# A fused attention and softplus kernel: new positions for all tasks and identity products, and a bank of its own for half of the last tile

## The chip, the cores and the metric

The kernel runs on one core of a Trainium2 chip. The core has TensorE (PE in the profile) with its weight loads (PEld), VectorE (DVE), ScalarE (ACT), GpSimd (POOL) and SyncE (SP, which here only issues DMAs). Matmuls write to PSUM, which the kernel uses as eight banks of 128 partitions x 512 float32 words; DVE and ACT read the banks.

The metric is the device time of one execution in microseconds, as the median of several runs. Lower is better.

## The reference

```python
kv = np.einsum('bhsd,bhse->bhde', k, v)          # B=8, H=8, S=576, D=64
out = np.einsum('bhsd,bhde->bhse', q, kv)
rms = np.sqrt(np.mean(out * out, axis=-1, keepdims=True) + 1e-06)
attn = (out / rms * g_norm).astype(np.float32)
x = attn.transpose(0, 2, 1, 3).reshape(B * S, H * D)      # 4608 x 512
h = x @ w_in                                     # 512 x 2048
g = np.maximum(h, 0.0) + np.log1p(np.exp(-np.abs(h)))     # softplus
return (g @ w_out).astype(np.float32)            # 2048 x 512
```

The weights w_in and w_out come as 64-bit floating point words, all else as 32-bit.

## The kernel before, in words

**Pieces.** A float32 operand is kept as three pieces of fewer bits (a high, a low and a third part, called `high`, `low` and `less` or `third` in the code) that TensorE takes. ACT makes the high part, DVE the two others. A logical product is therefore three matmuls for each 128 rows of depth.

**The head.** The first 60 us or so bring in and convert the first weights. A weight block `j` (even j: 128 columns of w_in, odd j: 128 rows of w_out) is fetched (L423), converted from 64-bit words by five DVE and two ACT operations (L433 to L465), and split into pieces (L498 to L529; for some blocks the third piece comes by way of two products on TensorE, L525 and L526). In the same time k and v are loaded (L683, L685) and multiplied batch by batch into kv (`kv_of`, L696), q tiles are loaded (L766) and transposed on TensorE (`turn_q`, L776), q is multiplied with kv (`out_rows`, L720), the rows are normed (square on ACT, sum on DVE L724, root on POOL L728, product on DVE L732), transposed (`turn_x`, L738), and split into pieces (L640, L643, L646). One of the 36 tiles of 128 rows is called `t`.

**Phase 0.** 64 steps (`step`, L849) follow. A step takes one block of 384 rows and one chunk of 128 hidden columns: 12 matmuls of 384 columns (`mm1`, L864), softplus on ACT (L886), pieces (L888, L875, L879), and three times 3 matmuls of 512 columns (`mm2`, L871) that add to a bank. Attention for later tiles is worked in between.

**Phases 1 and 2.** 48 wide steps (`wide_step`, L1044) take 512 rows and two chunks of hidden columns. The hidden part is made by seven products on half-sized blocks (`multiply`, L1066, 6 matmuls of 256 columns each) with sums between them: copies on ACT (L1091, L1108, L1112) and one DVE addition (L1116) on which the seventh product waits. Softplus (L1094) and pieces (L1124, L1127, L1130) follow, and then eight times 3 matmuls of 512 columns (`mm2`, L1137), for two chunks c and four tiles i. The last step's pieces are made chunk by chunk (L1152, L1154, L1158). In the last step of a block of 512 rows, `leave` (L913) takes each tile's sums out of its bank, scales them and sends them to the output. For the last tile of all, `leave` does this in two halves: `left` on ACT (L921), `right` on DVE (L924), both into the one output tile `ot`, followed by one DMA for each half (L928 on SP, L929 on ACT).

**What sets the order.** The program's order is written by a planner in Python (`Plan.order`) when the kernel is built. Every operation is a task with an engine, a nominal duration, the tasks that it depends on, the buffers that it takes and gives back, and a position. Where several tasks of an engine can start at about the same nominal time, the planner takes the one with the lowest position. The resulting lists are the instruction streams of the engines; each engine then runs its own in order. The positions come from lists of numbers: P0 for the weight blocks (conversion, fetch), P4 for the tiles' attention, P5 for k, v and q of the batches, P7 for single loads of k, v and q in the head, P1 and P2 for the later weights, P3 for the order inside a wide step.

**Identity products.** Where the planner finds TensorE without a task for 400 nominal ns or more before the seventh step of phase 0, it puts in a product of the identity with itself (`warm`, L1237: one matmul of 512 columns, into a bank of ring `h` that is free). Nothing reads its result.

Of the kernel before, what the change touches and what calls it, by code (L numbers as in the profile page):

```python
# [9 lines left out]
F32R = mybir.dt.float32r  # L10
# [3 lines left out]
ALU = mybir.AluOpType  # L14
# [4 lines left out]
P = 128  # L19
# [22 lines left out]
def from_the_end(x, w):  # L42

    return x.rearrange("p (b w) -> p b w", w=w)[:, ::-1] if w else x
# [16 lines left out]
class Plan:  # L61
# [13 lines left out]
    def __init__(self, rings, heirs):  # L75
        self.tasks = []
        self.rings = rings
        self.heirs = heirs
        self.spare = None

    def slot(self, ring):
# [12 lines left out]

    def order(self):
        waiting = {id(t): len(t.after) + (t.follows is not None) for t in self.tasks}
# [4 lines left out]
        ready = {}  # L101
# [25 lines left out]
        last_read = {}  # L127
        kind = "all"
        done, left = [], len(self.tasks)
        while left:  # L130
            best = None
            for engine, tasks in ready.items():
# [43 lines left out]
            for s in t.take:  # L176
# [30 lines left out]
def kernel(  # L207
# [48 lines left out]
    P4 = [-25.02, 20.2, -13.13, -76.26, -21.76, -10.12, -13.88, -3.49, -13.41, -2.4, 1.09, 2.92, -13.22, -8.15, 1.39, 9.36, 9.73, 7.7, 8.45, 45.46, 49.36, 108.95, 0.63, -0.65, 41.31, 39.36, -10.27, -9.48, 6.89, 16.18, -10.59, -3.45, 0.13, 22.43, -9.21, -44.87]  # L256
    P5 = [12.9, -1.7, -2.54, 10.43, -13.48, -0.41, 10.17, 0.5, 87.97, -18.71, 3.23, 0.27, -48.19, -4.24, -6.29, -0.07]
    P6 = [0.48, 3.29, 2.98, -0.03, -0.99, 3.23, 4.31, -4.05, 3.36, -3.53, 1.77, 4.22, -3.23, 9.1, 2.62, 10.18, 5.16, 0.22]
    P7 = [-28.31, -28.46, -11.62, -12.85, -9.89, -11.87, 32.22, 42.15, -30.41, -29.6, -3.37, 4.56, 17.98, 18.03, 4.6, 18.0, 19.05, 17.55, 18.65, 16.7, -11.69, -73.47, 123.81, 3.66, 5.87, 16.42, 9.28, 11.26, 20.7, 109.97]
    CONVERT, FETCH, EARLY, LATER = P0[:8], P0[8:16], P0[16:27], P0[27:]  # L260
    P1 = [47.61, 47.37, 57.59, 80.4, 121.52, 131.38, 22.92, 57.01, 70.7, 137.8, 137.94, 139.73]
    P2 = [26.2, 35.6, 23.56, 37.01, 50.1, 83.1, 74.5, 105.16, 106.57, 102.56, 158.35, 3.53, 130.79, 126.11, 174.6, 1.44, 158.35, 130.84, 184.62, 158.4, -7.15]
    P3 = [2.79, 2.5, 6.49, -0.11, 1.88, 3.37, 3.85, 0.39, 3.68, 3.69, 3.08, 2.2, 0.77, 1.98, 1.26, -2.35]
    SPLIT = {p: (P1[i], P1[6 + i]) for i, p in enumerate((2, 3, 4, 5, 6, 7))}
    TAKEN = {c: (P2[c - 6], P2[4 + c]) for c in range(6, 16)}
    LEAD, APART, AHEAD, MM2, LATE, SPLIT_G = P3[0], P3[1], P3[2], P3[3:11], P3[11:14], P3[14]
    EARLIER = P3[15]
    PACE = 2.5
    BY_PE = 12
    AT_ONCE = 2 * TB  # L270
# [639 lines left out]
        return add("DVE", 700, lambda: nc.vector.tensor_tensor(out=new(bank, [P, d_model]), in0=p0.tile, in1=p1.tile, op=ALU.add),  # L910
                   [l0, l1], pos, [bank], [p0, p1])

    def leave(ph, t, bank, done, pos):  # L913

        ot = slot("m")
        if ph == LAST and t == n_tiles - 1:
            mid = d_model // 2
            dst = out[t * P:(t + 1) * P]

            def left():  # L920
                nc.scalar.activation(new(ot, [P, d_model])[:, :mid], bank.tile[:, :mid], func=AF.Copy, scale=scale)  # L921

            def right():
                nc.vector.tensor_scalar(out=ot.tile[:, mid:], in0=bank.tile[:, mid:], scalar1=scale, scalar2=None, op0=ALU.mult)  # L924
# [4 lines left out]
            add("ACT", 100, lambda: nc.scalar.dma_start(out=dst[:, mid:], in_=ot.tile[:, mid:]), [b], pos, [], [ot], 400)  # L929
            return  # L930
        a = add("ACT", 690 if ph == LAST else 600, lambda: nc.scalar.activation(
            new(ot, [P, d_model]), bank.tile, func=AF.Copy, scale=scale if ph == LAST else 1.0),
            [done] + (scale_done if ph == LAST else []), pos, [ot], [bank])
# [12 lines left out]
        st = add("SP", 350, lambda: nc.sync.dma_start(out=dst, in_=ot.tile), [a], pos, [], [ot], 720)  # L946
        part.setdefault(t, []).append((dst, st))
# [96 lines left out]
    def wide_step(k):  # L1044
# [87 lines left out]
        def mm2(c, i):  # L1132
# [3 lines left out]
            for m in range(3):  # L1136
                nc.tensor.matmul(from_the_end(mine[i].tile, P), lhsT=(gvt(m, F32R) if m < 2 else gt(F32R))[:, c, i * P:(i + 1) * P],  # L1137
                                 rhs=from_the_end(outs[c].tile[:, m], P),
                                 start=fresh and not m, stop=(last and c == 1 and m == 2), skip_group_check=True)

        seeds = {}
        if first and ph == LAST:
            for i in range(TW):
# [91 lines left out]
    def warm(s):  # L1235

        nc.tensor.matmul(new(s, [P, 4, P]), lhsT=ident_r, rhs=ident_r.unsqueeze(1).to_broadcast([P, 4, P]),  # L1237
                         start=True, stop=True)

    plan.spare = ("h", warm, 400, mm1s[6][1])  # L1240
    for t in plan.order():
        t.run()
# [30 lines left out]
```

## Time and profile before

Three runs took 857.47, 858.39 and 860.43 us.

| what | value |
|---|---|
| median of the runs | 858.39 us |
| profiled execution, its own time | 858.92 us |
| its span in the trace | 857.1 us |
| PE busy | 843.8 us (98%) |
| DVE busy | 704.3 us (82%) |
| ACT busy | 520.7 us (61%) |
| POOL busy | 77.3 us (9%) |
| matmul instructions | 6470 |

Times in the profile are microseconds from the start of the span. An instruction row gives its start, its duration, engine, line, operation, what it writes and reads with the shapes, how many of a kind follow each other, and in brackets how long its engine had been idle and what ended that. The durations of pipelined matmuls overlap, so that a row of several is not the sum of single ones. A chain row gives start, length and line; the chain is the work that ended last, followed back from the end. Rows of DMA issues stand for the issue on the queue, not for the transfer.

### The profile page before, as it was taken

Reading aid. Unit: us, or ns where it says so; the run is one execution under the profiler, and the core shown is the slowest. Engines: PE = TensorE matmul, PEld = TensorE weight load, DVE = VectorE, ACT = ScalarE, POOL = GpSimd, SP = SyncE. Lnnn points to the kernel's source line nnn. Section 1 sums busy time; section 2 is a strip of 40 time slices with the busy share of each in tenths; the row PEclk is TensorE's granted clock in tenths of the full one; section 3 lists DMA queues with packets and bytes.
Section 4 is the critical chain, followed back from the end, with each engine's and each line's share of the span. In section 5 each row is a group of like instructions: output and inputs, shape, how many; then the busy total and the mean of one; then the engine's idle time right before and its main releaser. Section 6 shows DMA issues by size and latency. Waiting matters only on the chain.

```text
span 857.1 us, 17097 instructions
## 1 busy us (share of the span) xinstructions
PE 843.8 (98%) x6470; PEld 755.9 (88%) x6470; DVE 704.3 (82%) x998; ACT 520.7 (61%) x980; POOL 77.3 (9%) x79
## 2 busy tenths in 40 slices
PE   8899999999999999999999999999999999999998
PEld 6688888989898999999999999999999999999996
DVE  7998898888788889798888897897787866788873
ACT  5766664445444567776667665654868555666653
POOL 0343123111112200000000000000000000000000
PEclk9999999999999999999999999999999999999999
DMA  9998997779875655446654654735354654677764
GB/s 282 298 223 213 256 253 228 174 239 257 220 183 142 176 155 182 140 124 198 208 160 153 197 183 158 231 124 184 123 188 157 221 167 128 216 242 239 246 193 131
DMA packets 239628, 167.09 MB, mean 195 GB/s; under 512 B 106169, under 2 KB 198585, under 8 KB 239545
## 3 DMA queue, kind: packets, MB, share of 16 engines
q1 hardware_dynamic: 239392, 165.86, 65.6%
q8 instruction: 51, 0.84, 0.4%
q14 instruction: 33, 0.26, 0.1%
q10 hardware_dynamic: 152, 0.13, 0.0%
HBM read 112.98 MB, written 52.95 MB: 194 GB/s over the span
## 4 chain that ended last, share of the span: by engine, by line
PE 91%; DMA 2%; DVE 2%; ACT 1%; POOL 1%; SPq 1%; issue 1%; POOLq 0%; DVEq 0%; ACTq 0%
PE banks L1137 30%; PE banks L1066 27%; PE banks L871 14%; PE banks L864 14%; PE banks L720 2%; DMA loads<-in_v_dram 2%; PE banks L696 2%; POOL roots L728 1%; DMA g<-in_moe_w_out_dram 1%; DVE half L732 1%; SPq L685 1%; PE banks L738 0%; DVE roots L724 0%; POOL roots L727 0%; DVE units L643 0%
## 5 line engine op out<-in xcount | busy, mean ns | idle before, releaser
L1137 PE MATMUL banks<-pieces,gv 128*128 128x512 f32 x768 | 236.7, 389 | 0.0
L1137 PE MATMUL banks<-pieces,g_False 128*128 128x512 f32 x384 | 149.4, 389 | 0.0
L1137 PEld LDWEIGHTS banks<-pieces,gv 128*128 128x128 f32 x768 | 132.8, 188 | 17.5 <-DVE banks L910 0.2
L864 PE MATMUL banks<-units,pieces 128*128 128x384 f32 x768 | 144.7, 337 | 0.0
L871 PE MATMUL banks<-pieces,gv 128*128 128x512 f32 x576 | 143.4, 393 | 0.0
L864 PEld LDWEIGHTS banks<-units,pieces 128*128 128x128 f32 x768 | 134.7, 188 | 4.6
L871 PEld LDWEIGHTS banks<-pieces,gv 128*128 128x128 f32 x576 | 106.2, 188 | 18.9 <-DVE gv L879 0.3
L1066 PEld LDWEIGHTS banks<-units,pieces 128*128 128x128 f32 x840 | 110.2, 188 | 5.6
L1066 PE MATMUL banks<-units,pieces 128*128 128x256 f32 x840 | 114.0, 280 | 0.0
L1137 PEld LDWEIGHTS banks<-pieces,g_False 128*128 128x128 f32 x384 | 72.1, 188 | 15.0
L886 ACT ACTIVATE half<-banks 128x384 f32<-128x384 f32 x64 | 31.4, 491 | 86.7 <-PE banks L864 80.4
L1127 DVE TENSOR_TENSOR gv<-g_True,gv 128x1024 fp32r<-128x1024 f32 x47 | 57.5, 1224 | 28.0 <-ACT gv L1124 27.7
L1066 PEld LDWEIGHTS banks<-units,w 128*128 128x128 f32 x504 | 66.9, 188 | 3.8
L1066 PE MATMUL banks<-units,w 128*128 128x256 f32 x504 | 69.3, 280 | 0.0
L1116 DVE TENSOR_TENSOR g_True<-banks,g_True 128x512 f32<-128x512 f32 x48 | 33.2, 691 | 36.4 <-PE banks L1066 29.6
L728 POOL TENSOR_TENSOR roots<-roots,half 128x8 f32<-128x8 f32 x36 | 62.6, 1739 | 3.0
L1130 DVE SCALAR_TENSOR_TENSOR g_False<-gv 128x1024 fp32r<-128x1024 f32 x47 | 57.6, 1225 | 1.6
L1026 ACT ACTIVATE units<-loads 128x1024 fp32r<-128x1024 f32 x42 | 44.4, 1056 | 17.1 <-PE banks L1066 10.2
L1029 DVE TENSOR_TENSOR units<-loads,units 128x1024 fp32r<-128x1024 f32 x42 | 51.2, 1219 | 3.7 <-ACT units L1026 3.5
L1112 ACT COPY banks<-banks 128x256 f32<-128x256 f32 x48 | 17.3, 359 | 59.9 <-PE banks L1066 59.5
L1032 DVE SCALAR_TENSOR_TENSOR units<-units 128x1024 fp32r<-128x1024 f32 x42 | 51.4, 1224 | 1.7
L1124 ACT ACTIVATE gv<-g_True 128x1024 fp32r<-128x1024 f32 x47 | 49.9, 1061 | 1.5
(118 smaller groups left out, 1263.9 us busy)
## 6 DMA issues: line engine op xcount, KB each, us to landing
loads<-x SPq DMA_DIRECT2D x180, 128.0 KB, 2.5
part<-m SPq DMA_DIRECT2D x72, 256.0 KB, 2.7
m<-part SPq DMA_DIRECT2D x72, 256.0 KB, 3.3
loads<-form SPq DMA_DIRECT2D x45, 256.0 KB, 3.1
form<-loads SPq DMA_DIRECT2D x36, 256.0 KB, 2.7
raw<-in_moe_w_in_dram SPq DMA_DIRECT2D x16, 512.0 KB, 5.0
loads<-in_v_dram SPq DMA_DIRECT2D x32, 256.0 KB, 4.3
loads<-in_k_dram SPq DMA_DIRECT2D x32, 256.0 KB, 4.0
```

The lines of the kernel that those rows point to most:

```text
L728: nc.gpsimd.tensor_tensor(out=r.tile, in0=r.tile, in1=half, op=ALU.pow)
L864: nc.tensor.matmul(from_the_end(hp, w), lhsT=w_in.tile[:, i, kd * P:(kd + 1) * P], rhs=from_the_end(xv.tile[:, i, kd], w), start=(m == 0), ...
L871: nc.tensor.matmul(mine[i].tile, lhsT=gv.tile[:, m, i * P:(i + 1) * P], rhs=w_out.tile[:, m], start=(c == cs[0] and m == 0), stop=(c == cs ...
L1026: nc.scalar.activation(part_of(0, F32R), xl.tile if m > 1 else xl.tile[:, 0], func=AF.Copy, scale=DOWN)
L1029: nc.vector.tensor_tensor(out=part_of(1, F32R), in0=xl.tile if m > 1 else xl.tile[:, 0], in1=part_of(0), op=ALU.subtract)
L1032: nc.vector.scalar_tensor_tensor(out=part_of(2, F32R), in0=part_of(1), scalar=-RADIX, in1=part_of(0), op0=ALU.mult, op1=ALU.add)
L1066: nc.tensor.matmul(from_the_end(place(q), (16, 8)[kd]), lhsT=w[:, m, at:at + P], rhs=from_the_end(dst.tile[:, m, v, kd] if u < 6 else dst. ...
L1116: d = add("DVE", 700, lambda: nc.vector.tensor_tensor(out=gt()[:, :, HW:], in0=ab.tile[:, 1].rearrange("r (q t) -> r q t", q=2), in1=gt()[ ...
L1124: nc.scalar.activation(gvt(0, F32R), gt(), func=AF.Copy, scale=DOWN)
L1127: nc.vector.tensor_tensor(out=gvt(1, F32R), in0=gt(), in1=gvt(0), op=ALU.subtract)
L1130: nc.vector.scalar_tensor_tensor(out=gt(F32R), in0=gvt(1), scalar=-RADIX, in1=gvt(0), op0=ALU.mult, op1=ALU.add)
L1137: nc.tensor.matmul(from_the_end(mine[i].tile, P), lhsT=(gvt(m, F32R) if m < 2 else gt(F32R))[:, c, i * P:(i + 1) * P], rhs=from_the_end(ou ...
```

## The change

The change has three parts.

1. All lists P0 to P7 and P1 to P3 hold other numbers. This changes the order of tasks on the engines, that of the loads on SP included; no task is added or taken away by it, apart from the identity products that the planner puts where it finds TensorE idle.
2. A list `FILL` and a function `Plan.fillers`: ahead of the n-th task on TensorE, identity products not counted, for each n in the list one more identity product is put in, if a bank of ring `h` is free in the plan. Its nominal duration is zero, so that the plan's times stay.
3. The last tile of the last step. Its product for chunk 0 and tile 3 gets an earlier position. A new function `apart` has ACT copy the right half of that tile's bank to another bank (`aside`), and then runs the last product (chunk 1, tile 3) in two halves: three matmuls of 256 columns into the left half of the old bank, and three into `aside`. `leave` for this tile has `right` (DVE) read `aside`, after the right half's product; `left` (ACT) depends on the left half's product.

```diff
+    def fillers(self, count, since, at, free):
+        ring, run, _, _ = self.spare
+        places = [p for ready, p in sorted(free[ring]) if ready <= at]
+        made = []
+        for _ in range(self.fill.count(count) if places else 0):
+            s = Slot(ring)
+            s.place = places[0]
+            f = Task("PE", 0, lambda s=s: run(s), [], None, [s], [s], 0)
+            f.kind, f.start = "all", at
+            made.append(f)
+        return made
...
             if t.engine == "PE":
+                if t.pos is not None:
+                    done += self.fillers(count, engine_free["PE"], at, free)
+                    count += 1
...
-    P0 = [-24.73, -20.97, 0.27, 0.08, -28.09, -2.67, -1.41, 3.37, -97.07, -96.4, -79.24, -94.59, -21.66, -92.87, 1.06, -21.73, 23.09, -46.04, 5.54, 9.76, 6.68, 22.62, -12.61, 4.25, -1.18, 32.61, -14.32, 7.05, 6.28, 5.48]
+    P0 = [0.79, 2.33, -1.4, 0.04, -27.91, -2.89, -1.56, 3.6, -80.5, -88.95, -102.88, -14.89, -24.12, -13.91, 1.3, -16.31, 23.47, -45.74, 5.79, 9.76, 5.92, 23.36, -12.79, 4.17, 0.31, 24.52, -39.11, 6.35, 7.61, 5.35]
...
-    P3 = [2.79, 2.5, 6.49, -0.11, 1.88, 3.37, 3.85, 0.39, 3.68, 3.69, 3.08, 2.2, 0.77, 1.98, 1.26, -2.35]
+    P3 = [2.51, 2.65, 6.72, -0.3, 1.27, 3.2, 4.21, -1.72, 3.25, 3.09, 2.35, 1.87, 0.83, 0.63, 1.01, -2.4]
...
+    FILL = [11, 13, 14, 18, 19, 26, 40, 51]
...
-    def leave(ph, t, bank, done, pos):
+    def leave(ph, t, bank, done, pos, right_done=None, aside=None):
...
-                nc.vector.tensor_scalar(out=ot.tile[:, mid:], in0=bank.tile[:, mid:], scalar1=scale, scalar2=None, op0=ALU.mult)
+                nc.vector.tensor_scalar(out=ot.tile[:, mid:], in0=aside.tile[:, 1, :mid], scalar1=scale, scalar2=None, op0=ALU.mult)
...
             a = add("ACT", 390, left, [done] + scale_done, pos, [ot], [bank])
-            b = add("DVE", 430, right, [done] + scale_done, pos + 0.01, [], [bank], follows=a)
+            b = add("DVE", 430, right, [right_done] + scale_done, pos + 0.01, [], [aside], follows=a)
...
+        def apart(pos):
+
+            aside, bank = slot("ab"), mine[-1]
+
+            def half_of(to, at):
+                for m in range(3):
+                    nc.tensor.matmul(from_the_end(to(), P), lhsT=(gvt(m, F32R) if m < 2 else gt(F32R))[:, 1, (TW - 1) * P:],
+                                     rhs=from_the_end(outs[1].tile[:, m, at:at + HW], P),
+                                     start=False, stop=(m == 2), skip_group_check=True)
+
+            moved = add("ACT", 380, lambda: nc.scalar.copy(new(aside, None)[:, 1, :HW], bank.tile[:, HW:]), [before[TW - 1]], pos, [aside])
+            need = [split_done[1], moved, before[TW - 1]] + factors_done[1, 2 * p + 1]
+            a = add("PE", 350, lambda: half_of(lambda: bank.tile[:, :HW], 0), need, pos)
+            b = add("PE", 350, lambda: half_of(lambda: aside.tile[:, 1, :HW], HW), [a], pos, [], [gv, outs[1]])
+            leave(ph, n_tiles - 1, bank, a, pos, b, aside)
...
-                slot_pos = b + PACE + MM2[TW * c + i]
+                slot_pos = b + PACE + MM2[TW * c + i] - (6 if k == len(STEPS) - 1 and i == TW - 1 and not c else 0)
+                if c and k == len(STEPS) - 1 and i == TW - 1:
+                    apart(slot_pos + 2)
+                    continue
...
+    plan.fill = FILL
     plan.spare = ("h", warm, 400, mm1s[6][1])
```

P4, P5, P6, P7, P1 and P2 have other numbers in the same way. P6 holds the positions at which the pieces of x are made for the blocks of phases 1 and 2 (`units_of`).

More of the change, by code (lines that the diff above doesn't have):

```diff
@@ L79, in __init__ @@
         self.spare = None
+        self.fill = []
     def slot(self, ring):
@@ L129, in order @@
         done, left = [], len(self.tasks)
+        count = 0
         while left:
@@ L253 @@
     LAST = 2
-    P0 = [-24.73, -20.97, 0.27, 0.08, -28.09, -2.67, -1.41, 3.37, -97.07, -96.4, -79.24, -94.59, -21.66, -92.87, 1.06, -21.73, 23.09, -46.04, 5.54, 9.76, 6.68, 22.62, -12.61, 4.25, -1.18, 32.61, -14.32, 7.05, 6.28, 5.48]
-    P4 = [-25.02, 20.2, -13.13, -76.26, -21.76, -10.12, -13.88, -3.49, -13.41, -2.4, 1.09, 2.92, -13.22, -8.15, 1.39, 9.36, 9.73, 7.7, 8.45, 45.46, 49.36, 108.95, 0.63, -0.65, 41.31, 39.36, -10.27, -9.48, 6.89, 16.18, -10.59, -3.45, 0.13, 22.43, -9.21, -44.87]
-    P5 = [12.9, -1.7, -2.54, 10.43, -13.48, -0.41, 10.17, 0.5, 87.97, -18.71, 3.23, 0.27, -48.19, -4.24, -6.29, -0.07]
@@ L258 @@
-    P6 = [0.48, 3.29, 2.98, -0.03, -0.99, 3.23, 4.31, -4.05, 3.36, -3.53, 1.77, 4.22, -3.23, 9.1, 2.62, 10.18, 5.16, 0.22]
-    P7 = [-28.31, -28.46, -11.62, -12.85, -9.89, -11.87, 32.22, 42.15, -30.41, -29.6, -3.37, 4.56, 17.98, 18.03, 4.6, 18.0, 19.05, 17.55, 18.65, 16.7, -11.69, -73.47, 123.81, 3.66, 5.87, 16.42, 9.28, 11.26, 20.7, 109.97]
+    P0 = [0.79, 2.33, -1.4, 0.04, -27.91, -2.89, -1.56, 3.6, -80.5, -88.95, -102.88, -14.89, -24.12, -13.91, 1.3, -16.31, 23.47, -45.74, 5.79, 9.76, 5.92, 23.36, -12.79, 4.17, 0.31, 24.52, -39.11, 6.35, 7.61, 5.35]
@@ new lines @@
+    P4 = [-18.06, 19.14, -15.76, -77.96, -21.77, -12.91, -12.44, -5.37, -13.04, -3.62, 1.12, 2.49, -13.36, -16.79, 1.46, 11.74, 10.37, 6.03, -4.28, 41.0, 51.62, 54.84, 0.4, -8.79, 43.74, 43.68, -27.46, -7.67, 4.71, 16.59, -8.05, -0.14, 0.76, 9.19, -24.74, -8.02]
+    P5 = [8.92, -4.32, -2.61, 11.08, -9.33, -3.34, 7.1, -4.71, 96.42, 25.68, 2.79, 0.84, -47.93, -4.41, -3.45, -0.56]
+    P6 = [0.29, 1.55, -0.26, -0.54, -4.41, 3.0, 6.91, -25.58, 0.69, -4.45, 1.8, 5.54, 5.35, 0.74, -0.03, 5.63, 8.98, 5.11]
@@ L260 @@
+    P7 = [-22.4, -22.35, -15.68, -22.85, -7.92, 47.57, 50.43, 56.32, -17.43, -19.71, 13.65, 13.76, 13.71, 13.43, 16.08, 13.67, 19.16, 17.82, 19.71, 5.11, -22.35, -6.17, 79.76, 74.59, 19.2, 18.22, 11.69, 12.05, 20.18, 70.22]
     CONVERT, FETCH, EARLY, LATER = P0[:8], P0[8:16], P0[16:27], P0[27:]
-    P1 = [47.61, 47.37, 57.59, 80.4, 121.52, 131.38, 22.92, 57.01, 70.7, 137.8, 137.94, 139.73]
-    P2 = [26.2, 35.6, 23.56, 37.01, 50.1, 83.1, 74.5, 105.16, 106.57, 102.56, 158.35, 3.53, 130.79, 126.11, 174.6, 1.44, 158.35, 130.84, 184.62, 158.4, -7.15]
@@ L263 @@
-    P3 = [2.79, 2.5, 6.49, -0.11, 1.88, 3.37, 3.85, 0.39, 3.68, 3.69, 3.08, 2.2, 0.77, 1.98, 1.26, -2.35]
+    P1 = [47.72, 47.41, 57.41, 82.81, 116.42, 131.27, 17.63, 55.92, 72.81, 129.4, 159.48, 139.37]
+    P2 = [24.55, 35.57, 23.55, 37.06, 50.14, 82.78, 66.23, 108.93, 109.54, 123.42, 152.47, -1.01, 74.95, 131.82, 144.18, 0.74, 144.23, 150.66, 132.46, 131.87, -7.48]
+    P3 = [2.51, 2.65, 6.72, -0.3, 1.27, 3.2, 4.21, -1.72, 3.25, 3.09, 2.35, 1.87, 0.83, 0.63, 1.01, -2.4]
     SPLIT = {p: (P1[i], P1[6 + i]) for i, p in enumerate((2, 3, 4, 5, 6, 7))}
```

## The prediction

> **What bounds the kernel now.** I read the page first: busy times, slices, and the summary of the chain that ended last.
>
> ```profile
> span 857.1 us, 17097 instructions
> PE 843.8 (98%) x6470; PEld 755.9 (88%) x6470; DVE 704.3 (82%) x998; ACT 520.7 (61%) x980; POOL 77.3 (9%) x79
> PE   8899999999999999999999999999999999999998
> PEclk9999999999999999999999999999999999999999
> PE 91%; DMA 2%; DVE 2%; ACT 1%; POOL 1%; SPq 1%; issue 1%; POOLq 0%; DVEq 0%; ACTq 0%
> ```
>
> PE is busy for 843.8 of 857.1 us, at full granted clock, and is 91% of the chain. So all that an order of work can win lies in PE's idle 13.3 us and in products that compute nothing. Next, the table by stretches shows where those 13.3 us are (columns: stretch, its length, then busy time and count of PE, weight loads, DVE, ACT and POOL, then clock, DMA share and GB/s).
>
> ```profile
> 0.00:62.00 62.00, 53.67 (x671) 41.55 (x671) 53.01 (x96) 42.73 (x84) 18.39 (x23) 1.00 0.98 268
> 62.00:140.00 78.00, 76.79 (x819) 67.26 (x819) 69.30 (x119) 47.89 (x94) 22.70 (x20) 1.00 0.89 240
> 140.00:335.00 195.00, 195.00 (x1708) 176.38 (x1707) 165.08 (x285) 99.33 (x197) 36.21 (x36) 1.00 0.70 191
> 335.00:853.40 518.40, 518.37 (x3276) 470.73 (x3275) 416.43 (x500) 330.27 (x606) 0.00 (x0) 1.00 0.58 181
> 853.40:857.10 3.70, 0.00 (x0) 0.00 (x0) 0.48 (x1) 0.47 (x1) 0.00 (x0) 1.00 0.57 213
> ```
>
> PE idles 62.00 − 53.67 = 8.33 us in the head, 1.21 us from 62 to 140, 0.03 us over the next 713 us, and 3.70 us after its last product. The head is also where the identity products stand, and its DMA share is 0.98: the loads there queue behind each other. So there are three places to cost: head, steady part (where only a loss is possible), tail.
>
> **The head: identity products.** PE's waits and its identity products (L1237), from the head's timeline:
>
> ```profile
> 8.23 1.88 PE L1237 MATMUL banks<-ident_r 128*128 128x512 f32 x7
> 20.02 0.69 PE L696 MATMUL banks<-loads 128*64 128x64 f32 x16 [0.64 <-DMA loads<-in_v_dram]
> 22.44 1.16 PE L720 MATMUL banks<-early,w 64*64 64x64 f32 x64 [0.31 <-ACT early L704]
> 24.97 0.69 PE L696 MATMUL banks<-loads 128*64 128x64 f32 x16 [0.98 <-DMA loads<-in_v_dram]
> 29.31 0.66 PE L738 MATMUL banks<-ident_r,half 128*128 128x128 f32 x4 [0.80 <-DVE half L732]
> 31.66 0.69 PE L696 MATMUL banks<-loads 128*64 128x64 f32 x16 [0.80 <-DMA loads<-in_v_dram]
> 35.05 2.09 PE L1237 MATMUL banks<-ident_r 128*128 128x512 f32 x8
> 38.56 0.66 PE L776 MATMUL banks<-ident_r,w 128*128 128x128 f32 x4 [0.42 <-ACT w L802]
> 41.89 1.16 PE L720 MATMUL banks<-early,w 64*64 64x64 f32 x64 [0.57 <-DVE half L732]
> 60.17 0.66 PE L738 MATMUL banks<-ident_r,half 128*128 128x128 f32 x4 [1.01 <-DVE half L732]
> ```
>
> Eight products in 2.09 us and seven in 1.88 us make 0.26 to 0.27 each with the pipeline's fill, so about 0.24 for one more in a row. The two built programs have 58 before and 65 after: the planned ones fall by one and FILL adds eight. In the new order the eight stand ahead of the rows of tile 0 (wait 0.31), of the kv products that now wait 0.98 and 0.80, of three q transposes (one waits 0.42), and of two tasks near 52 and 60 us. An identity product of 0.24 us put ahead of a task that waits longer than that costs nothing, since it needs no data; ahead of one that doesn't wait it costs its 0.24 us, if PE isn't made to wait later anyway. The 1.01 us at 60.17 follow the filler near 52 us, the waits from 24.97 to 41.89 us follow most of the others, and only the last, behind the wait at 60.17, has no cover in these rows. I take **+0.24**. Bounds: 0 (all covered) and +1.9 (8 x 0.24, no cover left, should the loads come sooner). One planned product fewer gives up to −0.24, inside these bounds.
>
> **The head: the new order of tasks and loads.** Counted in the order of the issues, the loads of tile 0's q move ahead of more of the weights, the first weight fetches swap places (j2 ahead of j0), the later k and v loads of batch 2 move up, and the fetch of weight block j7 moves back, with 12864 KB ahead of it instead of 10496. For the kv products that wait at 20.02 and 24.97 us, the KB issued ahead of the later of their two loads stay the same, so these waits stay. For those at 31.66 us the later load has 128 KB less ahead of it; at the head's 268 GB/s this is 0.49 us. The task also waits for PE's own earlier work, so I take **−0.3** of it. Bounds: what DVE, which must convert all weights in the head, waits in 5 to 62 us:
>
> ```profile
> DVE half L732 <- POOL roots L728: 1.2, 3, 0.6
> DVE units L643 <- ACT w L802: 0.8, 1, 0.8
> DVE m L511 <- ACT pieces L503: 0.7, 1, 0.7
> DVE roots L724 <- ACT half L793: 0.5, 1, 0.5
> ```
>
> That is 3.2 us; DVE is otherwise busy (53.01 of the first 62 us, and it cannot begin before its first loads), and its order of the first 130 instructions barely changes. So −3.2 is the end on the side of a gain. On the other side, the fetch that moves back:
>
> ```profile
> 35.42 0.45 SPq L423 DMA_DIRECT2D g<-in_moe_w_out_dram  x1
> 58.38 0.42 DVE L438 TENSOR_SCALAR m<-g 128x512 uint32<-128x512 uint32 x1
> ```
>
> It was issued 23 us before DVE took it. 2368 KB more ahead of it are 9.0 us at 268 GB/s, so of the 23 us some 14 remain for its own transfer: no loss. The bound for a loss here is one more wait like the longest of PE's, +1.0. The transpose of tile 11 that moves four products ahead on PE, about 4 us, can only take the 1.21 us of idle time between 62 and 140 us; its own x is normed earlier too, and I take **−0.1** (bounds −1.21 and +0.3, the smallest wait above).
>
> **The steady part.** A wide step issues 7 products of 6 matmuls, 8 of 3, and follows the one before without a gap; two neighbours of the chain, and the DVE addition on which the seventh product (the later L1066 rows) depends:
>
> ```profile
> 460.26 2.80 PE banks L1066 x24
> 463.06 2.72 PE banks L1137 x12
> 470.60 2.80 PE banks L1066 x24
> 470.64 1.22 DVE L1029 TENSOR_TENSOR units<-loads,units 128x1024 fp32r<-128x1024 f32 x1
> 480.37 0.69 DVE L1116 TENSOR_TENSOR g_True<-banks,g_True 128x512 f32<-128x512 f32 x1
> 481.48 0.75 PE L1066 MATMUL banks<-turned,half 128*128 128x256 f32 x5
> ```
>
> A step takes 470.60 − 460.26 = 10.34 us. The addition ends at 481.06, the product starts at 481.48: 0.42 us to spare. The new order has the same pattern of products in a step; it differs by exchanges of neighbours in the steps at 358 to 380, 605 to 620 and 663 to 668 us. Followed by hand with the durations above, none of these brings a product ahead of what it needs. PE's work is the same, and PE cannot be more than busy: **0**, bounds 0 and +1.5 (two steps in which one DVE operation of 1.22 us comes ahead of the addition: 2 x (1.22 − 0.42)).
>
> **The tail.**
>
> ```profile
> 850.01 0.69 ACT L931 ACTIVATE m<-banks,scale 128x512 f32<-128x512 f32 x1 [4.19 <-PE banks L1137]
> 853.41 0.47 ACT L921 ACTIVATE m<-banks,scale 128x256 f32<-128x256 f32 x1 [0.67 <-PE banks L1137]
> 853.92 0.48 DVE L924 TENSOR_SCALAR m<-banks,scale 128x256 f32<-128x256 f32 x1 [5.78 <-ACT m L921]
> 854.43 0.35 ACTq L929 DMA_DIRECT2D out_dram<-m  x1
> L1112 ACT COPY banks<-banks 128x256 f32<-128x256 f32 x48 | 17.3, 359 | 59.9 <-PE banks L1066 59.5
> ```
>
> ACT takes the left half of the last tile, and DVE the right half only when ACT is done, although the product had ended for both. Removed: that wait, 853.92 − 853.41 = 0.51 us. Added: one ACT copy of 0.36 us (the L1112 row has the same shape). In the new order it stands ahead of the three whole-tile leaves and behind the last high part, so it falls into ACT's idle 4.19 us; the product of that tile that it waits for is now the second of its step's eight instead of the seventh. Nothing waits for the copy but the last products, 4 us later. If that cover were gone, 0.36 us would be paid. Added on PE: six matmuls of 256 columns for three of 512, 6 x 2.80/24 − 3 x 2.72/12 = 0.70 − 0.68 = +0.02. The left half is now ready 0.35 us before the right one, so ACT leaves the left at 853.1 and DVE the right at 853.4, and the right half's transfer, the last, starts 0.5 us sooner. I take **−0.51 + 0.02 = −0.49**; bounds: 0 (DVE waits for the left half even so and something else is late) and −0.51.
>
> The row shows the order but not its reason: both engines read one bank, and both write one output tile m. The Trainium skill ("PSUM — Partial Sum Buffer", section "PSUM bank collisions raise a hardware error") says that two engines at one bank at once is an error, reads by ScalarE and VectorE included, so that such accesses must be ordered by bank. By that rule the bank of its own frees DVE and the sum stands at −0.49; were the shared output tile the reason, only the left half's head start would be won, −0.35 + 0.02 = −0.33. No run here shows yet which.
>
> **The sum.** +0.24 − 0.3 − 0.1 + 0 − 0.49 = −0.65 us. The profiled execution took 858.92 us (its span of 857.1 and 1.8 around it), so it would take 858.27; it lay 0.53 above the median of the runs, 858.39, so the median comes to **857.7 us**. What a measurement of this kernel can tell from no change is about 0.3%, 2.6 us: faster means under 855.8, slower over 861.0.
>
> **The rivals.**
>
> *The head gains in full.* The new order ends all of DVE's 3.2 us of waits, and the conversions, and with them the first steps, come that much sooner: 858.39 − 3.2 − 0.49 + 0.24 = 854.9 us. For it speaks that PE's waits quoted for the head add up to 5.5 us, and that q's loads come sooner. Against it: the longest waits go by loads in a full queue whose KB ahead do not change, and POOL's row is a chain of dependent operations that no order shortens. Chance 0.24.
>
> *Steady steps stall.* The seventh product waits for the addition L1116, and the addition is queued on DVE behind one more operation of 1.22 us: 1.22 − 0.42 = 0.80 us a step, which nothing hides, as PE has no idle time there. It decides from four steps on: 857.7 + 4 x 0.80 = 860.9; with five it ends at 861.7, with ten at 865.7. The 0.42 us to spare and DVE's 416.43 busy of 518.40 us speak for it, the nearly unchanged order of DVE against it. Chance 0.16.
>
> *Little is won and the fillers are paid.* All eight are exposed and the tail gives −0.33: 858.39 + 1.9 − 0.33 = 860.0. For it speaks that no filler needs to stand where PE waits once loads come otherwise than planned; against it the waits of 0.31 to 1.01 us in the rows. Chance 0.15, within the bound.
>
> **How the numbers follow.** The forecast has 0.45, the paid fillers 0.15, both within 0.3%: 0.60 the same; 0.24 faster; 0.16 slower. The likeliest's own range is 856.2 to 859.4: the terms' bounds taken half way. To hold 8 in 10 the range reaches to the first rival's 854.9, leaving out half of its chance below, and to 861.7 in the second: 854.8 to 861.7.
>
> **What the changed profile would show.** Right: L1237 x65 and hardly more PE idle time than 8.33 us less the fillers' 1.9 in the first 62 us; DVE's last operation starting within 0.1 us of the last product, before ACT's left half could have held it; about 3.2 us after the last product instead of 3.70; a step still 10.34 us; a wait under 0.5 at the kv products that now start at 31.66. Wrong: PE waiting on DVE L1116 in rows after 335 us; a DVE wait for the fetch of j7; the first products of the steady part (L864) starting more than 1 us sooner or later than now; or DVE's last operation still released by ACT.

## The result

The changed kernel takes 861.27 us in the median of 15 executions (the kernel before 858.35 beside it): 1.0032 times the time before, with a 95% interval of 1.0021 to 1.0042. It is slower by 2.8 us, 0.3%. One of the 15 executions took 2758.93 us and is left out of the ratio; the median of the other 14 is 861.20. A second measurement of the same kernel gave 1.0021 (1.0012 to 1.0030). The profiled execution took 860.34 us, 0.9 under that median, as that of before lay 0.5 over its own; so the two traces differ by 1.4 us only, and show the kinds of loss better than their size.

The table by stretches of the changed kernel, cut where its last product ends (columns as before):

```profile
0.00:62.00 62.00, 53.48 (x673) 41.33 (x674) 51.92 (x94) 42.43 (x83) 18.40 (x23) 1.00 0.98 263
62.00:140.00 78.00, 76.78 (x819) 67.51 (x818) 69.00 (x119) 48.05 (x94) 22.52 (x20) 1.00 0.90 241
140.00:335.00 195.00, 195.00 (x1708) 176.23 (x1707) 165.89 (x286) 98.61 (x196) 37.20 (x37) 1.00 0.71 193
335.00:854.72 519.72, 519.72 (x3286) 472.17 (x3284) 416.47 (x501) 331.08 (x610) 0.00 (x0) 1.00 0.57 180
854.72:858.50 3.78, 0.00 (x0) 0.00 (x0) 0.48 (x1) 0.38 (x2) 0.00 (x0) 1.00 0.56 208
```

Between 62 us and the last product PE is as busy as before. The last product ends 1.35 us later (854.72 against 853.37), and the end of the span follows 3.78 us behind it, against 3.73: the tail won nothing. Most of the loss lies in the head, as the starts below show. The head's timeline on PE has two things in it that the trace of before has not:

```profile
9.29 0.69 PE L714 MATMUL banks<-loads 128*64 128x64 f32 x16 [1.08 <-DMA loads<-in_v_dram]
...
33.03 1.16 PE L738 MATMUL banks<-early,w 64*64 64x64 f32 x62
35.48 0.33 PE L738 MATMUL banks<-early,w 64*64 64x64 f32 x2 [1.29 <-issue]
35.73 0.66 PE L756 MATMUL banks<-ident_r,half 128*128 128x128 f32 x4
```

The first kv product waits for its loads until 9.29 us. And inside one row product, after 62 of 64 matmuls, PE stops for 1.29 us. It is released by "issue": no semaphore and no transfer of data that the profile shows ends that wait. In the transfers listed by queue, a packet of the instruction queue (q8, 16 KB) runs from 33.19 to 34.12 us; the corresponding packet of before runs from 28.90 to 29.83. The row for q8 is the same in the window from 28.8 to 29.9 us of before and in that from 33.1 to 34.2 us of after:

```profile
q8 instruction: 1, 0.02, 5.3%
```

Up to that stop the changed kernel is not behind. Its row product starts at 33.03 us, and the product in the same place of the order before at 33.55, although 50 identity products have run by then instead of 46. Behind the stop PE is late, and it still is when the steps begin. The rows of before, and then the first step of the changed kernel:

```profile
33.55 1.16 PE L720 MATMUL banks<-early,w 64*64 64x64 f32 x64
34.64 0.66 PE L738 MATMUL banks<-ident_r,half 128*128 128x128 f32 x4
43.67 4.47 PE L864 MATMUL banks<-units,pieces 128*128 128x384 f32 x24
```
```profile
44.74 4.45 PE L882 MATMUL banks<-units,pieces 128*128 128x384 f32 x24
```

The transposes behind the row product start 1.09 us later (35.73 against 34.64), the steps 1.07 us later, and the first product of the wide steps 1.14 us later (338.66 against 337.52). From there to the last product's end lie 516.06 us, before 515.85. So in this pair of traces 1.07 of the 1.35 us are there by the end of the head, and the stop is what puts PE behind.

The tail, from the timelines of ACT, DVE and SP in the changed kernel:

```profile
853.36 1.37 ACT L949 ACTIVATE m<-banks,scale 128x512 f32<-128x512 f32 x2 [1.35 <-PE banks L1155]
854.63 0.47 ACT L939 ACTIVATE m<-banks,scale 128x256 f32<-128x256 f32 x1
855.33 0.35 ACTq L947 DMA_DIRECT2D out_dram<-m  x1
...
854.81 0.48 DVE L942 TENSOR_SCALAR m<-banks,scale 128x256 f32<-128x256 f32 x1 [5.38 <-ACT m L949]
...
854.08 1.03 SPq L964 DMA_DIRECT2D out_dram<-m  x2
855.20 0.41 SPq L946 DMA_DIRECT2D out_dram<-m  x1
```

DVE starts 0.09 us after the last product, as forecast (the row names L949 as the releaser, which is inferred; the right half now starts beside ACT's left half, not behind it). The right half's transfer is issued 0.61 us after the last product instead of 1.06. But from that issue to the end of the span it now takes 858.50 − 855.33 = 3.17 us, before 857.10 − 854.43 = 2.67. Since the product of chunk 0 of the last tile moved forward, the tile ahead of it is finished only one product before the end; ACT leaves it until 854.73, its 256 KB are issued last of L964, until 855.11, and the left half follows on SP at 855.20.

### The profile page after: what moved, and what is told of

Its sections match the earlier page's. It is cut to its first block, busy times and chain, and to the rows that moved or that the text cites. A ratio compares the mean times of both kernels' runs of the same rounds, so it can differ in the third digit from the quotient of the medians.

```text
span 858.5 us, 17091 instructions
## 1 busy us (share of the span) xinstructions
PE 845.0 (98%) x6480; PEld 757.2 (88%) x6480; DVE 703.8 (82%) x998; ACT 520.6 (61%) x981; POOL 78.1 (9%) x79
## 4 chain that ended last, share of the span: by engine, by line
PE 90%; DVE 4%; DMA 2%; POOL 1%; ACT 1%; issue 1%; SPq 0%; ACTq 0%; DVEq 0%; POOLq 0%
PE banks L1155 30%; PE banks L1084 27%; PE banks L889 15%; PE banks L882 14%; PE banks L738 2%; PE banks L714 2%; POOL roots L746 1%; DMA m<-x 1%; DMA loads<-in_v_dram 1%; DVE half L750 1%; PE banks L756 1%; DVE roots L742 0%; DVE m L465 0%; SPq L703 0%; DVE m L482 0%
## 5 line engine op out<-in xcount | busy, mean ns | idle before, releaser
L1134 DVE TENSOR_TENSOR g_True<-banks,g_True 128x512 f32<-128x512 f32 x48 | 33.1, 691 | 35.5 <-PE banks L1084 30.6
L949 ACT ACTIVATE m<-banks 128x512 f32<-128x512 f32 x72 | 41.7, 595 | 17.8 <-PE banks L1155 11.4
L1112 ACT ACTIVATE g_True<-banks 128x256 f32<-128x256 f32 x96 | 36.8, 384 | 24.9 <-PE banks L1084 24.5
```

The lines of the kernel that those rows point to most:

```text
L1112: nc.scalar.activation(dst, src, func=AF.Softplus, scale=1.0 + E)
```

## The experiments

Theory R: PE stops at a fixed count of its instructions because their refill is late, and the fillers (the extra identity products) and positions have moved that point to where it costs. Rivals: F, each filler costs its own time; S, the order of the first loads makes everything behind it late; L, the new order of the loads costs as a whole. Experiments on the tail stand beside these.

**First set: parts of the change undone.** again is the changed kernel itself. nofill and short:

```diff
-    FILL = [11, 13, 14, 18, 19, 26, 40, 51]
+    FILL = []
```
```diff
     def warm(s):
+        warmed.append(s)
+        if len(warmed) <= 8:
+            return
         nc.tensor.matmul(new(s, [P, 4, P]), lhsT=ident_r, ...
```

notail leaves `apart` and the −6 out and lets `right` read the old bank, behind `left`.

> The changed kernel itself, for a second trace. Theory R (PE's instruction refill): in the first trace PE stops for 1.29 us inside the row product of one tile (33.03 to 35.48 us, released by nothing but its own issue), while a 16 KB packet of the instruction queue is late behind the loads; so the stop is there again, at the same instruction, 1 to 3 us long, and the time is 2 to 3.5 us over the kernel before. Rival (an accident of one execution): no stop at that place, and the 2.9 us come from elsewhere in the trace.

> The changed kernel without the eight extra identity products (FILL empty). Theory R: twelve PE instructions fewer stand ahead of the row product, so the same count of instructions is reached later and the stop shrinks under 0.5 us or moves behind that product; 1 to 2 us faster than the changed kernel. Rival F (the fillers cost their own 0.24 us each): 1 to 1.9 us faster as well, but the stop of 1.3 us stays in the trace. Rival L (the order of the loads alone makes it): less than 0.5 us faster.

> The changed kernel with the tail of before (one product for the last tile, both halves read from one bank, the order of the last step as before). If the tail's gain is eaten by the output transfers that now lie closer together: within 0.3 us of the changed kernel, with the last transfer's start later by 0.45 us and its flight shorter by about 0.5 us. If the predicted gain is real: 0.5 us slower than the changed kernel.

> The changed kernel with eight of the eleven first identity products left out: 16 PE instructions fewer ahead of everything, all else the same. Theory R: the stop goes by the count of PE's instructions, so it leaves the row product (16 instructions later is in the transposes and identity products behind it) or changes its length; 0.5 to 1.3 us faster than the changed kernel if the refill is asked for as early as now. Rivals F and L: no change beyond 0.3 us, since the products left out run before the first load has landed.

| run | median us | ratio to before (95%) |
|---|---|---|
| again | 860.32 | 1.0021 (1.0012 to 1.0030) |
| nofill | 861.22 | 1.0032 (1.0018 to 1.0045) |
| notail | 860.72 | 1.0027 (1.0015 to 1.0038) |
| short | 859.93 | 1.0018 (1.0004 to 1.0031) |

The stop is there in again, nofill and notail. From their timelines on PE, in that order:

```profile
36.59 0.33 PE L738 MATMUL banks<-early,w 64*64 64x64 f32 x2 [1.51 <-issue]
```
```profile
37.18 0.33 PE L756 MATMUL banks<-ident_r,half 128*128 128x128 f32 x1 [1.99 <-issue]
```
```profile
36.87 0.46 PE L738 MATMUL banks<-early,w 64*64 64x64 f32 x2 [2.07 <-issue]
```

In nofill it sits in another product, and the table by stretches from 0 to a moment inside the stop says why; after first, nofill second:

```profile
0.00:34.30 34.30, 28.80 (x344) 20.94 (x344) 28.29 (x55) 22.47 (x42) 5.44 (x11) 1.00 1.00 288
```
```profile
0.00:36.00 36.00, 29.08 (x344) 21.48 (x344) 29.51 (x56) 23.52 (x45) 5.42 (x11) 1.00 1.01 285
```

PE has executed 344 matmuls and 344 weight loads in both (with 16 semaphore instructions and a drain they are the 705 of the expectations). The stop goes with the count, not with the work. In these runs PE goes on 1.35 to 1.47 us after the instruction packet has ended. That is what R said. R also expected the stop to shrink without the fillers, and it did not: the packet itself was later, from 34.78 us. In again PE is 0.38 us behind the trace of before when the row product starts (33.93) and 2.21 us behind it after the stop (transposes at 36.85 against 34.64). The Trainium skill ("Runtime: NRT & Kernel Launch", section "Instruction fetch mechanics") says that engines take their instructions in blocks of 16 KiB, 256 instructions, the next being fetched while one executes, and that the cost is mostly hidden. The packet's size agrees; here the cost was not hidden.

A long stop has a second price. nofill's table around its stop, and of the 3.4 us soon after it:

```profile
34.90:37.20 2.30, 0.31 (x4) 0.07 (x3) 1.67 (x3) 1.18 (x3) 0.93 (x2) 1.00 1.07 298
38.10:41.50 3.40, 3.40 (x23) 2.35 (x22) 3.32 (x6) 2.72 (x6) 2.33 (x3) 0.50 0.93 246
```

The granted clock was 0.50 for 3.4 us. The same followed the stop of 2.07 us in notail, and did not follow those of 1.29 and 1.51 us. The Trainium skill ("TensorE: Matmul & The Clock Gate", section "HAM oscillation — how this bites in real kernels") gives idle gaps over about 3.4 us as what to avoid; here gaps of 1.99 and 2.07 us were enough. Length alone does not decide: waits of 2.20 us in again and 2.15 us in notail, which end near 11 us, were followed by the full clock. Of the 25 executions of the changed kernel (after and again), 16 had a mean clock below 0.9985; of the 134 of the kernel before beside all sets of runs, 40.

short, with 16 instructions fewer ahead, has no stop. Its median is 0.4 us under again's and 1.3 under that of the first measurement, inside their intervals. What the missing stop is worth can't be read from it, as its trace has other losses: waits of 3.48 and 2.53 us for loads, and a stretch at half clock from about 24 us. notail differs from the changed kernel by less than either interval; its last transfer takes 859.9 − 857.19 = 2.71 us again and it ends 3.76 us after its last product: the tail's two effects cancel, as its expectation put it.

**Second set: the start, the old positions, another tail.** first_old puts only the start of the changed kernel back, by ranks on each engine; first_new does the reverse on the kernel before:

```diff
-    for t in plan.order():
+    for t in again(plan.order(), {'SP': [0, 4, 7, 3, 2, 6, 1, 5, 9, 8], 'PE': ..., 'ACT': [0, 2, 3, 4, 5, 1]}):
```

old_fill is the changed kernel with the old lists P0 to P7 and P1 to P3. tail_both has these too, no FILL, and this in place of the new tail:

```diff
-        def apart(pos):
+        def apart(c, pos):        # halves for chunk 0 and for chunk 1; the copy ahead of both
...
-                slot_pos = ... - (6 if k == len(STEPS) - 1 and i == TW - 1 and not c else 0)
-                if c and k == len(STEPS) - 1 and i == TW - 1:
-                    apart(slot_pos + 2)
+                if k == len(STEPS) - 1 and i == TW - 1:
+                    apart(c, slot_pos + 2 * c)
```

> The changed kernel, with the first ten loads on SP in the order of before (first k and v ahead of q of tile 0 and of the first w_out block), the first kv product ahead of the first q transpose on PE, and ACT's copy of that transpose four places later, as before; all else as changed. Theory S (the start makes it: the first kv product comes 1.7 to 3.5 us later, its buffers come free later, and all loads behind it, the refill of PE's instructions too, are late by that): the first kv product at 7.6 us, no stop of PE inside the row product, and 858.3 to 859.2 us, at most 0.7 over the kernel before. Rival R (the refill is late for another reason, the later positions or the fillers): the stop of 1.3 us or more stays, 860 us or more.

> The kernel before, with nothing but its first ten loads, its first kv product and first q transpose, and ACT's copy in the order of the changed kernel. Theory S: 860 to 861.5 us, the first kv product at 9 to 11 us, and PE's refill late by about 4 us more than before. Rival R: within 0.5 us of the kernel before.

> All positions as before, with the eight extra identity products and the new tail. Theory S: fillers and tail cost nothing that can be seen: 858.2 to 859.0 us, no stop of PE in the row product. Rival F (each filler costs 0.24 us): 859.5 to 860.4 us.

> All positions as before, no extra identity products, and another tail: for the last tile both products of the last step are made in two halves, so that the order of the last step stays as before and the tile ahead of it leaves two products before the end, not one. If the gain of the changed tail is eaten by the transfer of that neighbour tile: from the last product's end to the end of the span 3.25 to 3.35 us instead of 3.73, and the median 0.4 us under the kernel before. If the last transfer's flight is longer for another reason: 3.7 us or more, as in the changed kernel.

| run | median us | ratio to before (95%) | first kv product at | stop of PE |
|---|---|---|---|---|
| first_old | 860.59 | 1.0018 (1.0006 to 1.0031) | 6.69 | 1.57 |
| first_new | 860.78 | 1.0019 (1.0004 to 1.0033) | 10.99 | none |
| old_fill | 859.37 | 1.0007 (0.9995 to 1.0019) | 7.59 | 1.04 |
| tail_both | 858.52 | 0.9996 (0.9983 to 1.0008) | 7.82 | 0.61 |

Theory S falls as the only cause: first_old has its first kv product sooner than before and still the stop, and 1.5 us lost. But first_new shows that the new start alone can cost as much, with no stop: in its trace the first kv product waits 1.81 us and the clock falls to 0.50 near 16 us, and 10 of its 11 executions had a mean clock below 0.9985. And the stop belongs to the old positions as well:

```profile
35.71 0.33 PE L738 MATMUL banks<-early,w 64*64 64x64 f32 x3 [1.04 <-issue]
```
```profile
35.50 0.44 PE L756 MATMUL banks<-ident_r,half 128*128 128x128 f32 x2 [0.61 <-issue]
```

(old_fill and tail_both.) The trace of before, in which the packet ended 4.97 us ahead of the need, is one without it; how many executions of that kernel are, one trace can't say. Why the packet is some 4 us later in most traces, with the transfers behind and ahead of it much the same, no run shows: the moment at which it is asked for is not in the trace.

old_fill and before differ by the fillers and the tail: 0.0007, not resolved. In the clock the fillers may show: 11 of 12 executions of old_fill had a mean of at least 0.9985, against 94 of 134 before and 8 of 12 in tail_both; with the new positions it was 9 of 25 with fillers and 2 of 10 without (nofill). The counts point one way but are small. In tail_both the end follows 3.50 us after the last product, 0.23 less than before; 3.25 to 3.35 was expected. The right half's transfer takes 856.2 − 853.32 = 2.88 us there, between 2.67 and 3.17. So with the neighbour tile left earlier, half of the gain is there in this trace.

**Third set: the stop taken away in its own place.** All identity products between the point where the refill should be asked for and that where it is needed are left out, 18 in the changed order, 16 in the old:

```diff
     for t in plan.order():
+        if t.engine == "PE" and t.pos is None:
+            spare_ones += 1
+            if 40 < spare_ones <= 58:        # 38 and 54 in the old order
+                continue
         t.run()
```

> The changed kernel without the 18 identity products that stand on PE from about 25.7 to 38 us, behind the point where the next refill of PE's instructions is asked for and ahead of the point where it is needed. PE then takes its 705th instruction about 36 instructions later in its work. Theory R (the stop at that count, together with a late refill, is a cause of its own): no stop in the trace, and 0.8 to 1.5 us faster than the changed kernel, 859.4 to 860.4. Rival W (the stop only stands where PE would have waited for loads, or for DVE, anyway): no stop, but no time won, 860.5 or more.

> The same, with the first loads, the first kv product and ACT's copy as before too. If the start and the refill are the two causes in the head, each enough by itself for most of the loss: within 0.6 us of the kernel before. If the later positions cost time in a third way: 1 us or more over the kernel before.

> The kernel before without the 16 identity products that stand on PE from about 25.5 to 37.2 us. Theory R: the stop, which shows in two of the four traces with the old order, can't come any more; the lowest times stay as they are and the median is 0.3 to 0.8 us under the kernel before. Rival W: no difference beyond 0.2 us.

> The old positions with the tail in which both products of the last tile are made in halves, and without those 16 identity products. By the two measured parts (the tail's 0.24 us and what the refill's stop costs in the mean): 0.4 to 1.0 us under the kernel before, no stop, and 3.5 us from the last product's end to the end of the span.

| run | median us | ratio to before (95%) | lowest and highest mean clock |
|---|---|---|---|
| gap_new | 860.59 | 1.0018 (1.0004 to 1.0032) | 0.990 to 0.998 |
| gap_first | 859.76 | 1.0018 (1.0007 to 1.0029) | 0.994 to 0.998 |
| gap_old | 860.35 | 1.0015 (1.0004 to 1.0027) | 0.991 to 0.998 |
| gap_best | 859.69 | 1.0015 (1.0003 to 1.0027) | 0.994 to 0.998 |

The stop at that count is gone in all four traces (gap_old has one of 0.54 us a block earlier, after 218 matmuls), yet nothing is faster than before. All 48 executions lost clock. gap_old's table, before and in the window:

```profile
26.00:30.40 4.40, 2.25 (x16) 1.56 (x14) 4.10 (x8) 3.48 (x8) 3.97 (x4) 1.00 1.06 306
30.40:33.80 3.40, 3.40 (x40) 2.49 (x38) 3.20 (x6) 2.43 (x5) 0.35 (x1) 0.50 1.08 319
```

PE busy for 2.25 of 4.40 us, then half the clock. The identity products there pay for themselves: the kernel before without them is 0.15% slower, and the lost clock is what the runs show beside it. This set could not tell R from W, since it exchanged the stop for the clock.

**Fourth set: eight products fewer early, in two blocks, so that no gap grows by more than about 1 us.** trim_new is the changed kernel with this; trim_first has the old start as well; trim_best and trim_fill are tail_both without and with FILL.

```diff
+            if spare_ones in [12, 13, 14, 15, 23, 24, 25, 26]:        # 15 to 18 and 25 to 28 in the old order
+                continue
```

> The changed kernel without eight identity products from two blocks between 6 and 15 us (four of seven, four of six), so that no gap there grows by more than 1 us and PE reaches its 705th instruction 16 instructions later in its work. Theory R (the stop at that count is a cause of its own): stop under 0.5 us, granted clock 1.0 in most runs, 859.3 to 860.0 us, 1 to 1.7 under the changed kernel. Rival S (the loads are late and everything waits for them): under 0.4 us won.

> The same, with the order of the first loads, the first kv product and ACT's first copy as before. If stop and start are the whole loss: 858.3 to 859.2 us, within 0.6 us of the kernel before. If the later loads' new order costs by itself: 859.5 us or more.

> The old positions, the tail with both products of the last tile in halves, and eight identity products fewer between 8 and 16 us. Theory R: the stop, 0.9 us in the trace of the same kernel with all identity products, is gone; 857.6 to 858.2 us, 0.4 to 1.0 under the kernel before. If the stop is no cause with the old order: 858.4 us, as with that tail alone.

> The same with the eight extra identity products. If they cost by bringing the 705th instruction forward: now 858.0 us or less, and the granted clock 1.0 in nearly all runs. If each costs its own 0.24 us in part: 858.6 to 859.4 us, as the old positions with the extra products did.

| run | median us | ratio to before (95%) | stop |
|---|---|---|---|
| trim_new | 860.20 (before: 859.18) | 1.0006 (0.9994 to 1.0018) | 0.64 |
| trim_first | 859.30 | 1.0000 (0.9989 to 1.0011) | 0.41 |
| trim_best | 858.89 | 0.9994 (0.9982 to 1.0005) | 3.59, one refill earlier |
| trim_fill | 858.75 | 0.9999 (0.9987 to 1.0012) | 0.21 |

All of this set, the kernel before too, ran some 0.6 us longer than the others, so the ratios are what counts. In trim_new the stop has moved on into a block of identity products, at the same count, and is half as long:

```profile
38.29 1.66 PE L1274 MATMUL banks<-ident_r 128*128 128x512 f32 x6 [0.64 <-issue]
```
```profile
0.00:37.80 37.80, 30.43 (x344) 22.02 (x344) 29.25 (x56) 23.25 (x45) 5.42 (x11) 0.91 0.96 276
```

Taking those eight products out wins 1.3 to 2.2 us on the changed kernel (from 1.0032 or 1.0021 to 1.0006; the intervals of the first and the last just meet no more, those of the second and the last overlap). How much of this is the shorter stop and how much something else that eight products change, no run separates. It is not the clock that was won: 8 of trim_new's 12 executions have a mean below 0.9985, in the trace from 9.6 to 16.4 us, where PE waits for its loads. With the old start the kernel is level with before. first_old and trim_first differ by the eight products alone: 1.0018 against 1.0000, 1.5 us, but in two sets and with intervals that overlap. Between trim_new and trim_first, the start, lie 0.5 us, less than their intervals. trim_best shows the stop at the refill before, after 217 matmuls:

```profile
29.90 0.59 PE L794 MATMUL banks<-ident_r,early 128*128 128x128 f32 x2 [3.59 <-issue]
```

Counted as above, with semaphore instructions and drain, 449 instructions have run before this stop, and 449 before that in gap_old. 705 − 449 = 256: the two places lie one block apart.

trim_best was expected 0.4 to 1.0 us under the kernel before, and trim_fill at 858.0 or less with the clock at 1.0 in nearly all executions. Both are level with before, and 8 and 6 of their 12 executions lost clock. No kernel that was tried is faster than before beyond its interval.

## Why the prediction was wrong

It forecast 857.7, a gain of 0.7 us that could hardly be told from no change, and the kernel got slower by 2.8 us. That the measured 861.27 lies inside the range of 854.8 to 861.7, near its end, is luck: none of the rivals had the reason.

- **The head, new order of tasks and loads (−0.3, bounds −3.2 and +1.0): the step that failed.** It priced each load by the KB ahead of it, and only for products that already waited. A gain of this kind came: up to 33 us PE is 0.52 us ahead in the trace. What the step put at nothing, without a reason, is PE's own instructions, which come over the DMA engines too, and with them the count at which PE must have the next block. The stop at that count, 1.29 us in the trace and 1.51 in again, leaves PE 1.09 and 2.21 us behind. The step also kept the first kv product, which did not wait in the trace of before, out of sight; it waits 1.08 us (after) and 2.20 us (again) now. Removing eight early products took 1.3 to 2.2 of the 2.8 us away; with the start as before too, the kernel is level with before. The bound of +1.0, one more wait like PE's longest, was too near: the stops are longer, and 3.4 us at half clock follow those of 1.99 and 2.07 us. How the 2.8 us divide between stop, start and clock is not shown. The stop also stands in the two traces with the old positions (1.04 and 0.61 us), and why the refill comes late stays open. The trace of before alone would not have told: it is free of the stop, and "issue" is 1% of the chain's summary in both.
- **The identity products (+0.24).** Their price was low: by the prediction's own rows one more in a row is 2.09 − 1.88 = 0.21 us, not 0.24, but one that stands alone takes 0.32 to 0.43 us from its start to that of the next task (29.56 to 29.88 and 23.82 to 24.25 in the changed kernel). That they cost time all the same, no run shows: nofill takes as long as the changed kernel, if with a longer stop; old_fill lies 0.85 us above tail_both, but trim_fill 0.14 under trim_best, all inside their intervals. What was not in the forecast is that each of them brings the count forward by two, and what such products do for the clock, which the prediction read as 1.00 from one execution: without 16 or 18 of them all 48 executions lost some of it.
- **The tail (−0.49).** The mechanism was right: DVE no longer waits for ACT, though both still write one output tile, so the shared output tile was not the reason. The failing term was the transfer behind it, taken as unchanged: its flight grew by 0.50 us. In notail, without the moved product, it takes 2.71 us, and in tail_both, where the neighbour tile leaves earlier, 2.88; so the late neighbour tile is at least a part of the reason. The prediction looked for what the moved product costs on PE, and not on the output queue. Net: +0.05.
- **The steady part (0).** PE is busy without a gap from 140 us to its last product in both traces, and the waits on L1134 (before: L1116) that the rival with stalled steps needs are absent. From the first wide step to the last product it takes 0.21 us more; no run was made for that.
- **j7 and the turned tile 11.** No wait of DVE for the late fetch shows. From 62 to 140 us PE idles for 1.22 us, before 1.21: the −0.1 did not come.
- **The rivals.** The gain in full had the sign wrong: the 3.2 us of DVE's waits are not what bounds the head when loads come later. Steady stalls did not occur. The paid fillers come nearest in number (860.0), but nofill, without them, is not faster.
- **The signs.** The 65 identity products came, DVE's start 0.09 us after the last product, and no wait at the kv products that now start at 31.10 us. The head's idle time did not fall (8.52 us against 8.33), and the end follows 3.78 us after the last product, not 3.2. One sign of being wrong came true: the first product of the steps starts 1.07 us later.

## What to carry to other kernels

Identity products are instructions too: in a stretch where the DMA queues are full, count an engine's instructions between refills, and look for waits that only "issue" ends, in several executions, as one trace can be free of them. Where such products hold the clock, do not clear a whole stretch: without 16 or 18 in one stretch all 48 executions lost clock, without eight in two blocks 31 of 48. Where a wait in a tail is removed, follow the transfers to the end of the span, not just the start of the last.

## What was not expected of the hardware

- PE's stop at a fixed count of its instructions: after 344 matmuls and 344 weight loads in ten of 18 traces with 0.2 to 2.1 us, and 256 instructions earlier in two, with 0.54 (gap_old) and 3.59 us (trim_best); in the first set's traces PE goes on 1.35 to 1.47 us after the 16 KB packet's end.
- The granted clock was 0.50 for 3.4 us after stops of 1.99 and 2.07 us (nofill, notail), and after PE had been busy for 2.25 of 4.40 us (gap_old). After stops of 1.29 and 1.51 us (after, again), and after waits of 2.20 and 2.15 us near 11 us (again, notail), it stayed at 1.00; what decides was not worked out.
